# A 128x64-tiled key turn, a reordered kv sum and an earlier mantissa step in a fused polysketch attention and GELU block

## The chip, the cores and the metric

The kernel runs on one core of a Trainium2 chip. The metric is the device time of one execution in microseconds, a median over several runs. The engines of the core work side by side, each through its own instructions in order: TensorE (PE: matmuls; PEld is its loading of weights), VectorE (DVE), ScalarE (ACT), GpSimd (POOL) and SyncE (SP), which issues most of the DMAs. Matmul results land in PSUM, from where ACT and DVE take them.

## The reference

The reference is a polysketch attention followed by a GELU block. Only what bears on the change is shown:

```python
def phi(x):                                   # x: 4 batches, 4 heads, 1088 tokens, 32
    a = np.einsum('rd,bhsd->bhsr', S1, x)     # sketch, r = 8
    b = np.einsum('rd,bhsd->bhsr', S2, x)
    return np.einsum('bhsi,bhsj->bhsij', a, b).reshape(*x.shape[:-1], r * r)
q_p, k_p = (phi(q), phi(k))
kv = np.einsum('bhsf,bhsd->bhfd', k_p, v)
z = np.sum(k_p, axis=2)
num = np.einsum('bhsf,bhfd->bhsd', q_p, kv)
den = np.einsum('bhsf,bhf->bhs', q_p, z)[..., None] + 1e-06
x = num / den                                 # then (4352, 128): heads side by side
h = x @ w_in                                  # 128 x 2048
g = 0.5 * h * (1.0 + erf(h * inv_sqrt2))
out = g @ w_out                               # 2048 x 128
```

The reference returns float32. Some inputs (S1, S2 and both weights) arrive in 64-bit floating point, and the kernel makes their float32 values from the two 32-bit words itself.

## The kernel before

**Tiling.** The 1088 tokens of a batch are 1024 main tokens (8 groups of 128) and a remainder of 64. The four batches' main tokens make eight chunks of 512 tokens, the four remainders a ninth, shorter one. Each chunk goes through 16 hidden tiles of 128 channels: a product with w_in (line 721), a GELU on ACT (line 728), and the products with w_out (line 858 for the first tiles of the first batch, line 807 in a form with fewer products for all later ones).

**Staging.** The program is written out in order: for each engine, the order of the text is the order of its instructions, and the framework adds waits on semaphores where one engine needs another's result. A first part, lines 892 to 961, brings the first batch as far as its first hidden products. A loop over steps then runs the hidden tiles, and hangs all later preparation (rounding of weights, keys and queries of later batches) onto given steps. The change touches the first part alone.

**What the first part does, in order.** The sketches S1 and S2 are made. Keys of batch 0 are turned, so that their dimensions lie on partitions, and multiplied by the sketch (`key_features`). The four heads go as two pairs, r = 0 and r = 1, and each pair's features are `k_p[0, r]`. DVE multiplies three of the four halves of the features, POOL one; POOL also copies the values v into a wider tile `v_aug[r]` with a column of ones (lines 345 and 351), so that kv and z come out of one sum. The first queries are expanded (line 543), copied by ACT (line 550) and multiplied by DVE (line 555).

Then the sum over tokens, kv, is built in one PSUM bank, `kv_bank`. `kv_first(ps, r, tokens)` (line 426) issues two products for each group of tokens, each with 64 columns of weights, one for the upper and one for the lower 64 rows of the bank. Line 917 sums four of the eight groups of the first head pair. Line 918 turns the remainder's keys (`key_turn_rem`, which calls `transposed`, line 333, and copies by ACT, line 335, into `kT_rem`). Line 919 sums the other four groups. Line 920 multiplies `kT_rem` by the sketch (line 408), copies one factor by ACT (line 412, `a_rem`) and multiplies by DVE (line 413, `k_p_rem`). Line 921 sums all eight groups of the second head pair, and line 922 adds the remainder (line 432), which closes the sum. ACT copies it out as `kz` (line 930). `key_turn_rem` has a second use later in the loop, for the other pair of batches.

Around this, the second chunk's queries are turned (line 928, on TensorE through line 333). After kz, `numerators_by_token` (line 656) makes numerators and denominators of chunk 0, in two parts of two token groups each, and `divide` (lines 673 to 679) divides them on DVE. `turn_half_apart` (lines 694 and 696) turns the result into `xT`. `first_hidden` (line 737) is the first product with w_in, and the loop continues with the next hidden tiles (line 721).

**Rounding of weights.** A weight piece of 64-bit numbers is turned into float32 by the class `Rounding` in steps: `low_words` (ACT, line 260), `exponent_fields` (DVE, line 268), `mantissa_fields` (DVE, line 273), `exponents` (ACT, line 279), `mantissas` (DVE, line 287), `signs` (DVE, line 292), `product` (DVE or POOL, line 297). `fields` calls the exponent and the mantissa step one behind the other. Pieces 0 and 1 of w_in have 256 columns each: piece 0 serves the hidden tiles 0 and 1, piece 1 the tiles 2 and 3. POOL makes the product of piece 0, DVE that of piece 1. For piece 1 the exponent step stands at line 939, before the numerators, and the mantissa step at line 951, behind the copies of the turned x. When the product of piece 0 is done, POOL clears one word each of two landing tiles (line 180), on which SP's loads of w_out wait.

**PSUM.** Three pools of banks, each with two buffers: `h_ps` for hidden tiles, `o_ps` for outputs (in the first part `kv_bank` and the remainder's bank), `w_ps` for all else. A hidden tile's product can start only when the GELU has read the bank of the tile two before it.

Of the kernel before, what the change touches and what calls it, by code (L numbers as in the profile page):

```python
# [8 lines left out]
FP = mybir.dt.float32  # L9
# [7 lines left out]
def kernel(  # L17
# [18 lines left out]
    pe, dve, act, pool, sp = nc.tensor, nc.vector, nc.scalar, nc.gpsimd, nc.sync  # L36
# [7 lines left out]
    J = S // 128  # L44
# [16 lines left out]
    att = ctx.enter_context(tc.tile_pool(name="att", bufs=2))  # L61
# [18 lines left out]
    def out_bank():  # L80
        return ops.tile([128, CW], FP, name="o_ps")
# [8 lines left out]
    rem = {n: big.tile([128, B // 2, H, D], FP, name=f"{n}_rem") for n in "kv"}  # L90
# [128 lines left out]
    ident = big.tile([128, 128], FP, name="ident")  # L219
# [107 lines left out]
    def transposed(ps, name, srcs, copy, midway=lambda: None):  # L327

        n = len(srcs) * 128
        for i, s in enumerate(srcs):  # L330
            if 2 * i == len(srcs):
                midway()
            pe.transpose(ps[:, i * 128:(i + 1) * 128], in_=s, identity=ident)  # L333
        t = att.tile([128, n], FP, name=name, bufs=1 if name == "kT_rem" else 2)
        copy(out=t, in_=ps[:, :n])
        return t
# [5 lines left out]
    kT, k_p, k_p_rem = {}, {}, {}  # L342
# [27 lines left out]
    def spread(out, a, b):  # L370

        n = a.shape[1]
        return dict(out=out, in0=a[:, :, :, None].broadcast_to([128, n, R, R]),
                    in1=b[:, :, None, :].broadcast_to([128, n, R, R]))
# [25 lines left out]

    def key_turn_rem(pair, ps, copy):

        kT["rem"] = transposed(ps[:, 256:], "kT_rem", [rem["k"][:, pair].rearrange("p h d -> p (h d)")], copy)

    def key_features_rem(pair, ps):

        for rows in (slice(0, 64), slice(64, 128)) if pair == 0 else (slice(0, 128),):
            pe.matmul(ps[rows, 384:448], lhsT=kT["rem"][:, rows], rhs=S12.rearrange("p h r -> p (h r)"), start=True, stop=True)
        k_p_rem[pair] = big.tile([128, H, R, R], FP, name=f"k_p_rem{pair}")
        ab = ps[:, 384:448].rearrange("p (h r) -> p h r", r=2 * R)  # L410
        a = att.tile([128, H, R], FP, name="a_rem")
        act.copy(out=a, in_=ab[:, :, 0:R])
        dve.tensor_mul(**spread(k_p_rem[pair], a, ab[:, :, R:2 * R]))
# [3 lines left out]
    def flat(features):  # L417
        return features.rearrange("p i j -> p (i j)")

    def kv_first(ps, r, tokens=range(J)):  # L420

        for i in tokens:

            ch, t, one = i // 4, i // 2 % 2, i % 2
            for c in range(NP):
                pe.matmul(ps[c * F:(c + 1) * F, r * 2 * D:r * 2 * D + C], lhsT=flat(k_p[0, r][:, t, c * 4 + ch * 2 + one]),  # L426
                          rhs=v_aug[r][:, c, i, :C], start=(r == 0 and i == 0), stop=False, skip_group_check=True)

    def kv_first_rem(ps):
        for r in range(2):  # L430
            for c in range(NP):
                pe.matmul(ps[c * F:(c + 1) * F, r * 2 * D:r * 2 * D + C], lhsT=flat(k_p_rem[0][:, 2 * c + r]),
                          rhs=v_rem_aug[0][:, 2 * c + r, :C], start=False, stop=True, skip_group_check=True)
# [256 lines left out]
    def turn_half_apart(n, i, banks):  # L690
        if i == 0:
            xT[n] = att.tile([128, CW], FP, name="xT", bufs=3)
        for j, ps in enumerate(banks):
            pe.transpose(ps[:, :128], in_=x_tok[n, i][:, j].rearrange("p h d -> p (h d)"), identity=ident)
        for j, ps in enumerate(banks):
            (by_act, by_dve)[j](out=xT[n][:, i * 256 + j * 128:i * 256 + (j + 1) * 128], in_=ps[:, :128])
# [219 lines left out]
    kv_bank = out_bank()  # L916
    kv_first(kv_bank, 0, (0, 1, 4, 5))
    key_turn_rem(0, banks[1], by_act)
    kv_first(kv_bank, 0, (2, 3, 6, 7))
    key_features_rem(0, banks[1])  # L920
    kv_first(kv_bank, 1)
    kv_first_rem(kv_bank)
    w_in = [Rounding(w) for w in w_in_sb[:2]]
    w_in[0].low_words()
# [11 lines left out]
    w_out = [Rounding(w, beside=b) for w, b in zip(w_out_sb[:2], w_in)]  # L936
    by_act(**late[0])
    w_in[1].low_words()
    w_in[1].exponent_fields()
    parts = [range(2), range(2, JC)]  # L940
    nd = [[hidden_bank(), hidden_bank()], [out_bank(), out_bank()]]
    for banks, tokens in zip(nd, parts):
# [5 lines left out]
        divide(0, banks, tokens, by_head_pair=True, den=by)  # L948
    for half, bank in enumerate((hidden_bank, out_bank)):
        turn_half_apart(0, half, [bank(), bank()])  # L950
    w_in[1].mantissa_fields()
    for half in range(2):
        first_hidden(0, half)
    expand_copy(1, 0)
# [88 lines left out]
    def turn_keys_rem(pair):  # L1043
        held["rem"] = work_bank()
        key_turn_rem(pair, held["rem"], by_act)
# [46 lines left out]
    for n in range(3, NCHUNK):  # L1092
# [3 lines left out]
        keys = n % 2 and b < B  # L1096
# [158 lines left out]
```

## Time and profile before

| | |
|---|---|
| time, median of 3 runs | 259.67 us (258.98, 259.67, 259.85) |
| the profiled execution's own time | 259.66 us |
| its span, first to last instruction | 257.9 us |
| TensorE busy | 253.9 us (98%), 2335 matmuls |
| DVE, ACT, POOL busy | 151.1, 115.3, 164.6 us |
| mean granted TensorE clock | 1.000 |
| the first part (lines 892 to 961) on TensorE | up to about 16 us |

The span is what the profile covers; 1.8 us lie around it. A busy share counts the time between start and end of an engine's instructions. Matmuls overlap with the ones behind them and their ends are modelled, so the starts of matmuls tell more than their busy time: the distance between two starts is what one of them costs. In the views, a line gives start and length in us, then engine, line of the kernel, operation, what is written from what, shape and count; in brackets stands the idle time of the engine before it and who ended it.

### The profile page before, as it was taken

To read this page: it belongs to the slowest core of one execution; us is meant where nothing else is said; L and a number is where in the kernel's file an instruction comes from. 1 tells how busy PE (TensorE), PEld (TensorE's weight loads), DVE (VectorE), ACT (ScalarE), POOL (GpSimd) and SP (SyncE) were. 2 spreads that over 40 slices of the span, in tenths; PEclk is the share of its full clock that TensorE was granted. 3 is DMA by queue.
4 is the path that set the end of the run, shared out by engine and by line. 5 is a ranking of instruction groups with operands and counts; after the bars stand their busy time and mean duration, and the time that the engine had idled before them with its cause. 6 is when DMAs were issued, how large, how long until landed. Compare 5 with 4: busy or idle time off the path is not lost.

```text
span 257.9 us, 5770 instructions
## 1 busy us (share of the span) xinstructions
PE 253.9 (98%) x2335; PEld 135.7 (53%) x2335; DVE 151.1 (59%) x313; ACT 115.3 (45%) x224; POOL 164.6 (64%) x173
## 2 busy tenths in 40 slices
PE   8999999999999999999999999999999999999995
PEld 7856444354444545444444455455544444445794
DVE  2786888969699997590178986399307000700330
ACT  4675777433626332543335332533444334433442
POOL 3404016799968778587758775787758777877300
PEclk9999999999999999999999999999999999999999
DMA  7469849820000101102000002000200200020020
GB/s 204 140 188 373 201 94 220 221 55 10 3 0 13 30 1 23 21 8 35 3 0 3 0 10 37 0 1 3 41 3 5 38 0 1 10 34 0 3 41 20
DMA packets 29594, 13.48 MB, mean 52 GB/s; under 512 B 21888, under 2 KB 27776, under 8 KB 29568
## 3 DMA queue, kind: packets, MB, share of 16 engines
q1 hardware_dynamic: 29392, 13.05, 20.8%
q8 instruction: 18, 0.29, 0.5%
q10 hardware_dynamic: 176, 0.07, 0.1%
q14 instruction: 8, 0.07, 0.1%
HBM read 10.88 MB, written 2.23 MB: 51 GB/s over the span
## 4 chain that ended last, share of the span: by engine, by line
PE 98%; ACT 0%; issue 0%
PE h_ps L721 45%; PE o_ps L807 33%; PE o_ps L858 5%; PE w_ps L855 3%; PE w_ps L437 1%; PE w_ps L890 1%; PE w_ps L578 1%; PE w_ps L633 1%; PE w_ps L543 1%; PE o_ps L426 1%; PE h_ps L737 1%; PE w_ps L978 1%; PE w_ps L656 0%; PE h_ps L333 0%; PE w_ps L333 0%; PE o_ps L382 0%
## 5 line engine op out<-in xcount | busy, mean ns | idle before, releaser
L721 PE MATMUL h_ps<-xT,w_in 128*64 128x512 f32 (+3 forms) x514 | 137.0, 576 | 0.0
L728 ACT ACTIVATE block<-h_ps 128x512 f32<-128x512 f32 (+1 forms) x128 | 73.1, 571 | 117.3 <-PE h_ps L721 115.3
L721 PEld LDWEIGHTS h_ps<-xT,w_in 128*64 128x64 f32 (+1 forms) x514 | 41.8, 142 | 30.6 <-issue 11.6
L807 PE MATMUL o_ps<-block,w_out 128*64 128x256 f32 x224 | 57.5, 379 | 0.0
L772 POOL TENSOR_TENSOR bits_low<-block 128x512 f32<-128x512 f32 x28 | 35.9, 1282 | 27.8 <-ACT block L728 27.8
L807 PEld LDWEIGHTS o_ps<-block,w_out 128*64 128x64 f32 x224 | 30.5, 137 | 38.1 <-issue 27.6
L773 POOL TENSOR_TENSOR bits_a<-block 128x512 f32<-128x512 f32 x28 | 35.8, 1277 | 12.0 <-ACT block L728 11.9
L822 DVE COPY sums<-o_ps 64x256 f32<-64x256 f32 x8 | 3.3, 417 | 60.7 <-PE o_ps L807 60.7
L774 POOL TENSOR_TENSOR bits_e<-bits_a,block 128x512 f32<-128x512 f32 x28 | 36.1, 1288 | 2.2
L775 POOL TENSOR_TENSOR bits_m<-block,bits_e 128x512 f32<-128x512 f32 x28 | 35.9, 1280 | 2.2
L807 PE MATMUL o_ps<-bits_low,small 128*64 128x256 f32 x112 | 28.8, 379 | 0.0
L807 PE MATMUL o_ps<-block,small 128*64 128x256 f32 x112 | 28.8, 379 | 0.0
L807 PE MATMUL o_ps<-bits_a,small 128*64 128x256 f32 x112 | 28.8, 379 | 0.0
L807 PE MATMUL o_ps<-bits_m,w_out 128*64 128x256 f32 x112 | 28.7, 379 | 0.0
L807 PEld LDWEIGHTS o_ps<-block,small 128*64 128x64 f32 x112 | 15.2, 137 | 17.9 <-issue 10.8
L807 PE MATMUL o_ps<-bits_e,small 128*64 128x256 f32 x112 | 17.0, 383 | 0.0
L858 PE MATMUL o_ps<-g,w_out 128*128 128x512 f32 (+1 forms) x34 | 16.5, 572 | 0.0
L807 PEld LDWEIGHTS o_ps<-bits_m,w_out 128*64 128x64 f32 x112 | 15.3, 137 | 0.0
L807 PEld LDWEIGHTS o_ps<-bits_a,small 128*64 128x64 f32 x112 | 15.2, 137 | 0.0
L807 PEld LDWEIGHTS o_ps<-bits_low,small 128*64 128x64 f32 x112 | 15.2, 137 | 0.0
L590 DVE STREAM_TRANSPOSE w_ps<-w_ps 128x512 f32<-128x512 f32 (+1 forms) x7 | 4.8, 688 | 17.0 <-ACT xT L644 12.7
L807 PEld LDWEIGHTS o_ps<-bits_e,small 128*64 128x64 f32 x112 | 7.6, 137 | 10.6 <-issue 8.8
(195 smaller groups left out, 305.8 us busy)
## 6 DMA issues: line engine op xcount, KB each, us to landing
block<-in_moe_w_in_dram SPq DMA_DIRECT2D x3, 512.0 KB, 6.8
block<-in_moe_w_out_dram SPq DMA_DIRECT2D x3, 512.0 KB, 12.1
k<-in_k_dram SPq DMA_DIRECT2D x12, 128.0 KB, 2.9
v<-in_v_dram SPq DMA_DIRECT2D x12, 128.0 KB, 3.3
q<-in_q_dram SPq DMA_DIRECT2D x24, 64.0 KB, 2.3
out_dram<-oT SPq DMA_DIRECT2D x21, 64.0 KB, 2.2
k<-in_k_dram SPq DMA_DIRECT2D x2, 256.0 KB, 2.8
q<-in_q_dram SPq DMA_DIRECT2D x2, 256.0 KB, 3.8
```

The source lines that it names most:

```text
L426: pe.matmul(ps[c * F:(c + 1) * F, r * 2 * D:r * 2 * D + C], lhsT=flat(k_p[0, r][:, t, c * 4 + ch * 2 + one]), rhs=v_aug[r][:, c, i, :C], s ...
L590: dve.transpose(out=tok, in_=ps[:, :, :H2])
L721: pe.matmul(ps[rows, :W], lhsT=w[:, rows], rhs=xT[n][:, :W], start=True, stop=True)
L728: act.activation(out=g_of[n, fi][:, :W], in_=ps[:, :W], func=ACT.Gelu)
L772: pool.tensor_sub(out=s[3], in0=a11, in1=a21)
L773: pool.tensor_add(out=s[1], in0=a21, in1=a22)
L774: pool.tensor_sub(out=s[2], in0=s[1], in1=a11)
L775: pool.tensor_sub(out=s[4], in0=a12, in1=s[2])
L807: pe.matmul(acc[n][bank][half * 64:(half + 1) * 64, col:col + HW], lhsT=fixed, rhs=moving, start=opens and e == 0 and name in "4715", stop ...
L822: dve.tensor_copy(out=N[lo, 0, one], in_=a0[lo, one])
L855: pe.matmul(o_of[n][i][:, :128], lhsT=g[:, i * 128:(i + 1) * 128], rhs=w_tile(w_out_sb, fi), start=first, stop=final)
L858: pe.matmul(o_of[n][:, cols], lhsT=w_tile(w_out_sb, fi), rhs=g[:, cols], start=first, stop=final)
```

## The change

There are two edits in the first part, and one in a helper.

First, `mantissa_fields` of w_in's piece 1 moves on DVE from behind the copies of the turned x to just behind `exponent_fields`, which puts it ahead of the division of chunk 0.

Second, the first use of `key_turn_rem` (pair 0) no longer issues one transposing matmul of the whole 128x128 array. It issues two ordinary products with the identity, of 64 weight columns each, for the upper and the lower 64 rows of the bank. The copy by ACT stays. The later use (pair 1) stays as it was.

Third, four of the eight token groups of the second head pair's kv are summed before the remainder's sketch, and four behind it.

```diff
     def key_turn_rem(pair, ps, copy):
 
-        kT["rem"] = transposed(ps[:, 256:], "kT_rem", [rem["k"][:, pair].rearrange("p h d -> p (h d)")], copy)
+        keys = rem["k"][:, pair].rearrange("p h d -> p (h d)")
+        if pair:
+            kT["rem"] = transposed(ps[:, 256:], "kT_rem", [keys], copy)
+            return
+
+        for rows in (slice(0, 64), slice(64, 128)):
+            pe.matmul(ps[rows, 256:384], lhsT=keys[:, rows], rhs=ident, start=True, stop=True)
+        kT["rem"] = att.tile([128, 128], FP, name="kT_rem", bufs=1)
+        copy(out=kT["rem"], in_=ps[:, 256:384])
...
     key_turn_rem(0, banks[1], by_act)
     kv_first(kv_bank, 0, (2, 3, 6, 7))
+    kv_first(kv_bank, 1, range(4))
     key_features_rem(0, banks[1])
-    kv_first(kv_bank, 1)
+    kv_first(kv_bank, 1, range(4, J))
     kv_first_rem(kv_bank)
...
     w_in[1].low_words()
-    w_in[1].exponent_fields()
+    w_in[1].fields()
     parts = [range(2), range(2, JC)]
...
         turn_half_apart(0, half, [bank(), bank()])
-    w_in[1].mantissa_fields()
     for half in range(2):
```

## The prediction

> **What bounds the kernel.** I read first the chain of work that ended last and the busy time by stretches, then the timeline of the stretches that the edits touch. The page's chain:
>
> ```profile
> PE 98%; ACT 0%; issue 0%
> ```
>
> and one stretch (columns: us, then busy time of PE, PEld, DVE, ACT, POOL with instructions, PE's granted clock, DMA share, GB/s):
>
> ```profile
> 24.00:140.00 116.00, 116.00 (x953) 55.23 (x953) 85.58 (x158) 54.91 (x100) 80.24 (x79) 1.00 0.25 57
> ```
>
> TensorE sets the end, and from 24 us on it never runs dry. Both edits lie before 17 us, so the question is by how much TensorE's stream reaches 24 us earlier or later; the rest carries that offset. A busy PE can hide short waits, because matmuls overlap, so I go by their starts. The timeline around the first edit (start, length, engine, line):
>
> ```profile
> 8.66 0.66 PE L426 MATMUL o_ps<-sums,k_p 128*64 128x33 f32 x16
> ...
> 8.77 1.07 ACT L550 COPY A_sb<-w_ps 128x512 f32<-128x512 f32 x2 [0.61 <-PE w_ps L543]
> 9.14 0.61 POOL L345 COPY sums<-v 128x512 f32<-128x512 f32 x1
> ...
> 9.25 0.33 PE L333 MATMUL o_ps<-ident,k_rem 128*128 128x128 f32 x1
> ...
> 9.51 0.66 PE L426 MATMUL o_ps<-sums,k_p 128*64 128x33 f32 x16
> ...
> 9.73 0.28 ACT L335 COPY kT_rem<-o_ps 128x128 f32<-128x128 f32 x1
> ...
> 10.06 0.34 PE L408 MATMUL o_ps<-S,kT_rem 128*64 128x64 f32 x4
> ...
> 10.23 1.08 PE L426 MATMUL o_ps<-sums,k_p 128*64 128x33 f32 x32
> 10.45 0.19 ACT L412 COPY a_rem<-o_ps 128x32 f32<-128x32 f32 x1 [0.43 <-PE o_ps L408]
> ...
> 10.66 0.42 DVE L413 TENSOR_TENSOR k_p_rem<-a_rem,o_ps 128x256 f32<-128x256 f32 x1
> ...
> 11.23 0.42 PE L432 MATMUL o_ps<-v_rem_aug,k_p_rem 128*64 128x33 f32 x8
> ...
> 12.18 0.44 PE L656 MATMUL h_ps<-kz,q_pT 64*64 64x33 f32 x16
> ```
>
> See the sketch of the remainder at 10.06 (L408), its copy at 10.45, its product on VectorE at 10.66 to 11.08, and the kv product that needs it at 11.23 (L432). Then the copy kz, the numerators at 12.18, the division, the turn of x and the first hidden product at 15.07 follow, each on the one before.
>
> **The tiled turn.** Two 64-column products go in pairs: 16 pairs from 10.23 take 1.08, less the 0.22 of the last, over 15 pitches: 0.057 us a pair. Eight pairs from 8.66 are out of the way by 9.13, yet the turn starts at 9.25 and the next product at 9.51: with both changes of the array's tiling it costs 0.38. The new form, two 128x64 products with 128 moving columns, is not in this trace. A product is two MATMULs (16 for 8 calls at 8.66), a turn one. At line 543 a pass of 256 columns has a pitch of 0.215 (from 13.24, 1.12 less 0.37 for three pitches, the first longer), so 128 columns are 0.11 and two paired passes 0.22; bounds are 0.12 (33-column pairs, twice 0.057) and 0.44 (four passes not paired). I take 0.22, as the neighbours visibly pair; no change of tiling is left. TensorE gains 0.16 here (bounds -0.06 to 0.26): the second half of the first pair's kv starts at 9.35, not 9.51.
>
> The Trainium skill, "TensorEngine Tiling (Array Packing)", section "Restrictions", says that column tiling rules out the transpose mode for float32, which speaks against this edit. By that alone the turn doubles from 0.11 to 0.22, and the sum below would be 0.11 + 0.16 = 0.27 us worse than with my value; the two gaps around the turn in the row say why I don't go by it.
>
> Who profits? The copy kT_rem at 9.73 has its source at 9.58, but ScalarE's two A_sb copies run from 8.77 to 9.84 with an overlap: the copy goes when ScalarE is free. So kT_rem still lands at 10.01; the earlier turn brings the sketch nothing.
>
> **Half of the second pair's kv ahead of the sketch.** Eight pairs, 8 x 0.057 = 0.46. First half's rest from 9.35 to 9.81, then these eight to 10.27. Their inputs are there (v_aug by POOL at 9.14 + 0.61 = 9.75), with 0.06 to spare. But their first product waits on two engines, and a second wait is an instruction of its own in the weight queue: before L432, the 16 pairs from 10.23 end at 11.15 and the product starts at 11.23, 0.08 lost. Before the change this fell into the sketch's own wait; now it is paid, so the sketch goes at 10.35. The sketch's second pair, whose end frees the copy, was at 10.17 (0.057 before 10.23) and is now at about 10.41. So the sketch is **0.24 us later**. Bounds: 0.06 (turn at 0.12, no price for the wait) to 0.53 (unpaired turn, 0.22; POOL's copy 0.07 late).
>
> Queued behind it are ScalarE's copy a_rem (it waited for L408 at 10.45), the w_in steps behind that copy, the VectorE product L413 and all behind it. VectorE was free at 10.67, when L413 could start: there is no slack, all of it moves by 0.24, L432 to 11.47. TensorE has done the last eight pairs by 10.41 + 0.06 + 0.46 = 10.93 and then waits half a microsecond, where it waited 0.08. The query turn, kz, the numerators and the first hidden product move by the same 0.24; POOL's product of w_in's first piece too (12.44 + 0.75 = 13.19, needed at 15.07), and the gated loads that it holds on SP's queue, whose first result is used at 18.04.
>
> **The mantissa step** (L273) goes from behind the turned copies of x to just behind the exponent step, ahead of the division:
>
> ```profile
> 12.31 0.29 DVE L268 TENSOR_SCALAR bits_e<-small 128x256 uint32<-128x256 uint32 x1
> ...
> 12.89 0.23 DVE L673 TENSOR_SCALAR den_tok<-h_ps 128x4 f32<-128x4 f32 x2 [0.29 <-PE h_ps L656]
> ```
>
> VectorE idles 0.29 there for TensorE. One step started 0.20 behind L268 (11.00, 11.20) and takes 0.29: done at 12.80, before 12.89. It is hidden; without that cover the division would be up to 0.20 late. It waits for nothing new, since L268 read the same piece. What it leaves, and the weights that follow:
>
> ```profile
> 15.39 0.28 DVE L273 TENSOR_SCALAR bits_a<-small 128x256 uint32<-128x256 uint32 x1
> ...
> 15.70 0.42 DVE L287 SCALAR_TENSOR_TENSOR bits_m<-bits_a,bits_low 128x256 f32<-128x256 uint32 x1
> ...
> 16.03 2.99 PE L721 MATMUL h_ps<-xT,w_in 128*128 128x512 f32 x6
> ...
> 16.23 0.60 ACT L728 ACTIVATE g<-h_ps 128x512 f32<-128x512 f32 x1
> 16.50 0.42 DVE L297 TENSOR_TENSOR w_in<-bits_m,bits_e 128x256 f32<-128x256 f32 x1
> ...
> 17.04 0.30 PEld L721 LDWEIGHTS h_ps<-xT,w_in 128*128 128x128 f32 x2 [0.81 <-ACT g L728]
> ```
>
> w_in's second piece is ready at 16.92, and 0.31 earlier (15.70 - 15.39) after the change. The third hidden product waits for it: its weights load at 17.04 and it starts at 17.07, though the second, two passes of 0.43 from 16.03, was through at 16.89. It can't gain the whole 0.31: the bank it writes is free only when the first gelu ends, 16.23 + 0.60 = 16.83, and from there weights (0.05 behind a release, as L408 at 10.06 behind the copy's end at 10.01) and product (0.03) make 16.91. Gain **0.16** (bounds 0 and 0.23, the latter if also the slow restart after a wait went: 17.07 to 17.57 is 0.50 for a pass of 0.43). The later uses have cover: the query features end at 18.12 and are used at 18.95; w_out's first piece moves with VectorE, ahead of its use at 20.02.
>
> **Sum**, against the profiled execution: +0.24 - 0.16 = +0.08 us at 18 us and so at the end; bounds 0.06 - 0.23 = -0.17 and 0.53. Its span 257.9 becomes 258.0; what lies around it is 259.66 - 257.88 = 1.78, so 259.74. That execution is 0.01 below the median of the runs shown (259.67); I say **259.7**.
>
> **Rivals.**
> - *The remainder's chain has slack and TensorE keeps its gains*: 0.16 at the turn, 0.09 of wait before L408 (9.51 + 0.46 against 10.06), 0.08 before L432, 0.16 at the mantissa step: -0.49, 259.2. For it: the page shows no idle PE here. Against: the copy a_rem waited on L408 and L432 started 0.15 after VectorE's product.
> - *Unpaired turn, and the mantissa gains nothing*: +0.53, 260.2.
> - *Slower beyond doubt, by the clock*: the half microsecond of idle TensorE at 10.9 drops it to half speed. The trace shows such a speed: four 128-column turns take 1.06 from 3.78 and 0.66 from 11.59. It decides if the array falls back within 0.55 us; were it to stay so for the 5.7 us that the slow start lasts (0.77 to 6.47), half of them is lost: +2.9, 262.6. Against: waits of up to 0.18 pass here at full pitch.
>
> The Trainium skill, "TensorE: Matmul & The Clock Gate", Part 1, has the array go back to half rate only after a whole idle window of about 3.4 us. By it this rival is worth nothing; no run here shows the window.
>
> **Chances.** What a measurement can tell from no change is about 0.3%, 0.78 us; the three runs spread over 0.87, so that two medians may differ by it now and then. Forecast (259.7): 0.60, of it 0.05 reads faster and 0.04 slower by scatter. Slack: 0.22, of it 0.05 faster. Unpaired: 0.13, of it 0.03 slower. Clock: 0.05, slower. Faster 0.10, same 0.78, slower 0.12. The range reaches down past 259.2 by 0.3 of scatter and up past 260.2 by 0.3: 258.9 to 260.5.
>
> **What would show it.** Right: four MATMULs for the turn with the next kv product some 0.2 behind, L408 near 10.35, L432 near 11.47 behind an idle stretch, L273 ahead of the division, the third hidden product straight behind the second, and everything at 24 us within 0.2 of before. Wrong: L432 at or before 11.23, the division later than its numerators, or any new wait past 24 us.

## The result, and the profile after

| | before | after |
|---|---|---|
| median | 259.33 us (258.85 to 260.20, 22 runs) | 259.86 us (259.32 to 260.20, 22 runs) |
| the profiled execution's own time | 259.66 us | 260.2 us |
| its span | 257.9 us | 258.4 us |
| mean granted TensorE clock | 1.0 | 1.0 |

The ratio is 1.0016, with a 95% interval of 1.0009 to 1.0023: about 0.41 us slower (0.53 by the two medians), which is within 0.3% of no change. The changed kernel's profiled execution is the slowest of its 22. Of all executions in this study one was slow, 379.82 us at a granted clock of 0.66 in the combined kernel further down, and it is left out of that kernel's ratio. The forecast of 259.7 us lies 0.16 us below the measured median. The 22 runs of the kernel before have a median 0.34 us under that of the three runs shown at first, though, so against them the forecast difference of 0.08 us is short by some 0.33 us. That third of a microsecond is the subject of what follows.

In the changed kernel the lines from the sketch on are 8 higher (the sketch 408 is now 416, the kv products 426 are 434, the remainder 432 is 440, the denominators 673 are 681, the hidden products 721 are 729), and those from the new kv line to the old place of the mantissa step 9; the tiled turn is line 409 and its copy 411; lines below 400 keep their numbers.

The chain of work that ended last, in the changed kernel, by engine:

```profile
PE 95%; DMA 2%; DVE 0%; SPq 0%; ACT 0%; issue 0%
```

and the stretch from 24 to 140 us (busy time of PE, PEld, DVE, ACT and POOL, clock, DMA share, GB/s):

```profile
24.00:140.00 116.00, 116.00 (x952) 55.39 (x952) 85.37 (x159) 54.94 (x100) 79.25 (x79) 1.00 0.25 58
```

TensorE still never runs dry behind 24 us, and so the difference is made ahead of it. TensorE's timeline there:

```profile
8.81 0.66 PE L434 MATMUL o_ps<-sums,k_p 128*64 128x33 f32 x16
9.29 0.42 PE L409 MATMUL o_ps<-ident,k_rem 128*64 128x128 f32 x4
9.54 1.07 PE L434 MATMUL o_ps<-sums,k_p 128*64 128x33 f32 x32
10.45 0.32 PE L416 MATMUL o_ps<-S,kT_rem 128*64 128x64 f32 x4
10.59 0.61 PE L434 MATMUL o_ps<-sums,k_p 128*64 128x33 f32 x16
11.60 0.42 PE L440 MATMUL o_ps<-v_rem_aug,k_p_rem 128*64 128x33 f32 x8 [0.39 <-DVE k_p_rem L421]
```

The turn now is four MATMULs, and the next kv product follows 0.25 behind it. Sixteen pairs then stand ahead of the sketch instead of eight, and the remainder's kv product waits visibly for VectorE, which it did before for a moment only. The first kv product itself starts at 8.81 here and at 8.66 before. That start moves from one execution to the next with the landing of the inputs: over all profiles of this study it lies between 7.87 and 8.81. So the stages are counted from it here:

| us behind the first kv product | before | after | difference |
|---|---|---|---|
| sketch of the remainder | 1.406 | 1.639 | +0.233 |
| remainder's kv product | 2.573 | 2.788 | +0.215 |
| numerators | 3.516 | 3.729 | +0.213 |
| division | 4.236 | 4.803 | +0.567 |
| first hidden product | 6.407 | 6.874 | +0.467 |
| third hidden product | 8.410 | 8.763 | +0.353 |
| first hidden product past 24 us | 15.424 | 15.808 | +0.384 |
| end of the span | 249.220 | 249.592 | +0.372 |

This reads as two separate events. The key edits cost 0.21 and nothing more is added up to the numerators. Between numerators and division another 0.354 appears, of which 0.10 is absorbed by the first hidden product and 0.114 comes back at the third. The 0.372 at the end and the 0.15 by which the first kv product starts later make up the 0.5 us between the two profiled spans. The timeline of the other engines between numerators and division, where 0.354 is lost:

```profile
12.63 0.29 DVE L268 TENSOR_SCALAR bits_e<-small 128x256 uint32<-128x256 uint32 x1
...
12.80 0.73 POOL L297 TENSOR_TENSOR w_in<-bits_m,bits_e 128x256 f32<-128x256 f32 x1 [2.68 <-DVE bits_e L292]
12.84 0.85 DVE L273 TENSOR_SCALAR bits_a<-small 128x256 uint32<-128x256 uint32 x1
...
13.61 0.22 DVE L681 TENSOR_SCALAR den_tok<-h_ps 128x4 f32<-128x4 f32 x2
```

L273 is the moved mantissa step. At its old place it took 0.28 (line 273 at 15.39 in the profile before); here it takes 0.85, and shows no wait. It ends at 13.69, some 0.15 behind POOL's product, which began 0.04 ahead of it. The denominators (L681), the first step of the division, come behind the long instruction, where before they waited for TensorE. All of this is the reading of one execution of each kernel; the experiments ask whether it is the cause.

### The profile page after: what moved, and what is told of

Its sections match the earlier page's. It is cut to its first block, busy times and chain, and to the rows that moved or that the text cites. A ratio compares the mean times of both kernels' runs of the same rounds, so it can differ in the third digit from the quotient of the medians.

```text
span 258.4 us, 5777 instructions
## 1 busy us (share of the span) xinstructions
PE 253.3 (98%) x2338; PEld 135.7 (53%) x2338; DVE 151.5 (59%) x313; ACT 115.2 (45%) x224; POOL 163.5 (63%) x173
## 4 chain that ended last, share of the span: by engine, by line
PE 95%; DMA 2%; DVE 0%; SPq 0%; ACT 0%; issue 0%
PE h_ps L729 45%; PE o_ps L815 33%; PE o_ps L866 5%; PE w_ps L863 3%; DMA q<-in_q_dram 2%; PE w_ps L445 1%; PE w_ps L586 1%; PE w_ps L641 1%; PE w_ps L551 1%; PE h_ps L745 1%; PE o_ps L434 1%; PE w_ps L986 1%; PE w_ps L664 0%; SPq L100 0%; PE w_ps L333 0%; DVE qT L536 0%
```

## The experiments

Times are given as the median of the kernel, the ratio to the kernel before on the same chip and its 95% interval. An interval of 0.001 either way is 0.26 us, as large as most of what is asked for here; the traces resolve hundredths, but of one execution each. Both are given, and where they don't agree it is said.

**The parts alone.** Four kernels take the change apart. The first holds the key edits without the mantissa step, as against the changed kernel:

```diff
-    w_in[1].fields()
+    w_in[1].exponent_fields()
...
         turn_half_apart(0, half, [bank(), bank()])
+    w_in[1].mantissa_fields()
```

> The changed kernel with the mantissa step back in its old place; the turn in 128x64 tiles and the half kv sum ahead of the sketch stay. Times below are counted from the first kv product, since the two profiles reach it 0.15 us apart. In the changed kernel the remainder's kv product starts 0.215 us later than before, the numerators 0.213, and the first hidden product in steady order (at 24 us) 0.384. Theory K (the sketch moved back): remainder's kv product, numerators, division and first hidden product all 0.21 later than before, and 0.21 at 24 us; time about 0.2 us (0.08%) above before. Rival (all of the loss is the mantissa step's, the key edits cost nothing once the division is not disturbed): 0.0 to 0.05 at 24 us, time as before.

The second holds the mantissa step alone, as against the kernel before:

```diff
-    w_in[1].exponent_fields()
+    w_in[1].fields()
...
-    w_in[1].mantissa_fields()
```

> The kernel before with the mantissa step moved ahead of the division and nothing else. In the changed kernel that step took 0.852 us where it takes 0.282 in its old place, and it ran from 12.84 to 13.69 beside POOL's product of w_in's first piece, 12.80 to 13.54. Theory L (VectorE and POOL shut each other out there): here too the step takes 0.75 to 0.9 us and ends some 0.15 behind POOL's product, the division starts 0.3 to 0.4 later than before, and 0.15 to 0.2 stays at 24 us: time 0.06% above before. Rival D (in the changed kernel the step was long because the key edits had pushed it into something else, or because its input came late): here it takes 0.28 to 0.30, the division starts as before, and 0.16 us is gained at 24 us, as the prediction had it.

The third has the tiled turn, with the old order of the kv sums and the mantissa step at its old place (against the changed kernel):

```diff
-    kv_first(kv_bank, 1, range(4))
     key_features_rem(0, banks[1])
-    kv_first(kv_bank, 1, range(4, J))
+    kv_first(kv_bank, 1)
```

> The kernel before with the remainder's turn in two 128x64 tiles, and nothing else: all of the second pair's kv behind the sketch. In the changed kernel the turn and its next product came 0.085 us closer than before. Theory K: the sketch still waits for ScalarE's copy of the turned keys, which waits for ScalarE's two copies before it; sketch within 0.02 of before, remainder's kv product within 0.03, 24 us within 0.03, time as before. Rival (the tiled turn itself costs or gains on the path): remainder's kv product 0.05 or more away from before, and the same at 24 us.

The fourth has the new order with the old turn (against the kernel before):

```diff
+    kv_first(kv_bank, 1, range(4))
     key_features_rem(0, banks[1])
-    kv_first(kv_bank, 1)
+    kv_first(kv_bank, 1, range(4, J))
```

> The kernel before with four token groups of the second pair's kv ahead of the sketch, the turn in one transposing product, and nothing else. Theory K: the sketch comes 0.30 us later (0.213 as in the changed kernel and the 0.085 that the tiled turn gave back there), and so do the remainder's kv product, the numerators and the hidden products; time 0.3 us (0.12%) above before. Rival (the later sketch is absorbed behind it): the remainder's kv product later by 0.2 or more, but under 0.1 left at 24 us.

Differences to the kernel before, in us from the first kv product, and the times:

| | sketch | numerators | division | first hidden | third hidden | past 24 us | time, ratio (95%) |
|---|---|---|---|---|---|---|---|
| key edits alone | +0.428 | +0.407 | +0.407 | +0.406 | +0.405 | +0.405 | 259.47, 1.0002 (0.9992 to 1.0012) |
| mantissa step alone | +0.001 | -0.001 | +0.344 | +0.244 | +0.131 | +0.160 | 259.31, 0.9995 (0.9985 to 1.0004) |
| tiled turn alone | -0.014 | -0.013 | -0.013 | -0.012 | -0.011 | -0.011 | 259.41, 0.9995 (0.9974 to 1.0017) |
| order alone | +0.397 | +0.376 | +0.375 | +0.375 | +0.377 | +0.378 | 259.74, 1.0009 (1.0000 to 1.0018) |

The tiled turn is worth nothing by itself, as there was nothing behind it that could use the time. The order alone costs 0.38 and the changed kernel's numerators 0.21: the tiled turn gives 0.164 back once the order is such that TensorE's stream decides when the sketch goes (the second pair's first kv product stands 1.336 behind the first kv product with the old turn and 1.172 with the new one, in the changed kernel).

The mantissa step alone makes the division 0.344 late, with numerators that start at the same place to 0.001. VectorE and POOL in that kernel:

```profile
11.88 0.73 POOL L297 TENSOR_TENSOR w_in<-bits_m,bits_e 128x256 f32<-128x256 f32 x1 [2.47 <-DVE bits_e L292]
11.92 0.84 DVE L273 TENSOR_SCALAR bits_a<-small 128x256 uint32<-128x256 uint32 x1
...
12.68 0.22 DVE L673 TENSOR_SCALAR den_tok<-h_ps 128x4 f32<-128x4 f32 x2
```

Again POOL begins 0.04 ahead of L273, and L273 ends 0.15 behind POOL. So it is the mantissa step itself, and not the key edits around it, that makes the division late. This trace also holds a pause of TensorE inside the numerators (last section); a pause of that size put the division 0.145 late in another run, and the repeat of this one, without a pause, has the division 0.363 late.

The key edits alone gave +0.41 where the changed kernel has +0.21. Its timeline says why (TensorE, and POOL's copy of the second pair's values v):

```profile
8.04 0.66 PE L434 MATMUL o_ps<-sums,k_p 128*64 128x33 f32 x16
...
8.72 0.61 POOL L345 COPY sums<-v 128x512 f32<-128x512 f32 x1
8.78 1.27 PE L434 MATMUL o_ps<-sums,k_p 128*64 128x33 f32 x32
...
9.87 0.31 PE L416 MATMUL o_ps<-S,kT_rem 128*64 128x64 f32 x4
```

POOL's copy ends at 9.33, 1.29 behind the first kv product; in the changed kernel's profile it ended 1.09 behind it. The second pair's first product was due at 1.172 and went at 1.346, 0.05 behind the copy; in a later run with the copy at 1.375 it went at 1.428, again 0.05 behind. So the new order also brings a dependence on that copy into the chain, and in executions where the copy is late another 0.2 to 0.3 is paid. A repeat shows that it comes and goes:

> The key edits alone a second time, for a second profile and more times. In the first one TensorE reached the first kv product 0.6 us earlier than in the profile before, and there the second pair's kv waited for POOL's second copy of v. Theory K with POOL's copy: 0.21 at 24 us where POOL's copy is through before the second pair's kv begins, up to 0.41 where it isn't; time 0.2 to 0.4 us above before (0.08% to 0.16%). Rival (the delay from the first kv product is made up at the end, as the first times, 259.47 against 259.52, would have it): no difference in time again.

The repeat had the sketch at +0.233 and the numerators at +0.211, exactly as the changed kernel (259.55 us, 1.0010, 1.0001 to 1.0018). It lost another 0.45 inside the numerators, of which more below, and so stood at +0.67 past 24 us. The first run's time, within 0.31 of the kernel before by its interval, also suggests that its +0.405 in the trace isn't what most executions pay.

**How much can stand ahead of the sketch.** Two of the second pair's groups instead of four, without the mantissa step:

```diff
-    kv_first(kv_bank, 1, range(4))
+    kv_first(kv_bank, 1, range(2))
     key_features_rem(0, banks[1])
-    kv_first(kv_bank, 1, range(4, J))
+    kv_first(kv_bank, 1, range(2, J))
```

> Tiled turn, with two token groups of the second pair's kv ahead of the sketch and six behind it, mantissa step in its old place. In the changed kernel with four groups the sketch started 1.639 us after the first kv product, before it 1.406 behind ScalarE's copy; a group takes 0.117. Theory K (the sketch is late by what stands ahead of it beyond that copy): two groups end at 1.639 - 0.233 = 1.406, so the sketch starts within 0.03 of before, or up to 0.15 later where POOL's second copy of v is late; the remainder's kv product and 24 us likewise, 0.0 to 0.05 (0.15). Rival (any kv product of the second pair ahead of the sketch costs the whole): 0.2 or more.

Sketch, remainder and numerators are at -0.001 each (259.55 us, 1.0008, 0.9993 to 1.0023; a pause inside the numerators, as in the repeat above, put the rest at +0.14). None ahead gives -0.014 (+0.001 in the combined kernel below), two groups -0.001, four +0.233: TensorE has room for two groups while ScalarE's copies run, and the other two are on the chain in full (four pairs of 0.057, 0.23).

**Is it POOL's product that holds the mantissa step?** If it is, L273 must take its 0.28 when the product can't start ahead of it. A copy of one word of the step's result on POOL, just ahead of the product, makes the product follow it. First with the mantissa step alone, then with the whole change (the diff is against the changed kernel; the loads behind the product move with it):

```diff
     w_in[0].signs()
+    by_act(**late[0])
+    w_in[1].low_words()
+    w_in[1].fields()
+    pool.tensor_copy(out=mark, in_=w_in[1].a[:1, :1].bitcast(FP))
     w_in[0].product(pool)
     load_w_out(0, gated=True)
     load_rest()
     w_out = [Rounding(w, beside=b) for w, b in zip(w_out_sb[:2], w_in)]
-    by_act(**late[0])
-    w_in[1].low_words()
-    w_in[1].fields()
```

> The kernel before with the mantissa step moved ahead of the division, and POOL's product of w_in's first piece held back until that step is done (POOL copies one word of the step's result first; the gated loads stay behind the product). In the run with the mantissa step alone the step took 0.842 us and the division started 0.344 later, counted from the first kv product. Theory L (the two shut each other out while POOL's product runs): the step takes 0.28 to 0.30 again, the division starts within 0.03 of before, the first hidden product too, the third hidden product starts 0.15 earlier and 0.12 to 0.20 is gained at 24 us; POOL's product ends near 4.9 us after the first kv product, ahead of its use at 6.4. Theory D (the step is long by itself in that place): it stays at 0.8 us and the loss of 0.16 at 24 us stays.

> The changed kernel with POOL's product of w_in's first piece held back until the moved mantissa step is done. Theory L with K: the key edits' share stays (0.21 us at the numerators, up to 0.41 where POOL's second copy of v is late, counted from the first kv product), the division starts with the numerators again, and the third hidden product and 24 us are 0.15 earlier than with the key edits alone: 0.05 to 0.25 above before. Theory D: 0.38 or more above before at 24 us, as in the changed kernel.

VectorE and POOL with the mantissa step alone and the product held (one line more ahead of them, so that the step is L274 and the product L298):

```profile
11.83 0.28 DVE L274 TENSOR_SCALAR bits_a<-small 128x256 uint32<-128x256 uint32 x1
...
12.18 0.18 POOL L937 COPY mark<-bits_a 1x1 f32<-1x1 f32 x1 [2.65 <-DVE bits_a L274]
...
12.32 0.72 POOL L298 TENSOR_TENSOR w_in<-bits_m,bits_e 128x256 f32<-128x256 f32 x1
12.34 0.23 DVE L674 TENSOR_SCALAR den_tok<-h_ps 128x4 f32<-128x4 f32 x2 [0.23 <-PE h_ps L657]
```

The step takes 0.285, and the division waits for TensorE again, not for VectorE. What runs beside the product now are the division's instructions, the first at 0.23, as they did in the kernel before (L673 at 12.89 inside POOL's 12.44 to 13.19). So it is not any VectorE work that the product stretches.

| | sketch | numerators | division | first hidden | third hidden | past 24 us | time, ratio (95%) |
|---|---|---|---|---|---|---|---|
| mantissa step, product held | -0.014 | -0.013 | +0.080 | +0.079 | -0.098 | -0.075 | 259.34, 0.9996 (0.9987 to 1.0004) |
| whole change, product held | +0.510 | +0.490 | +0.490 | +0.536 | +0.361 | +0.385 | 259.45, 1.0003 (0.9994 to 1.0011) |

In the second of them POOL's copy of v was late again (1.375 behind the first kv product), which puts the numerators at +0.49. From there it tells the same: the division adds 0.000, where the changed kernel adds 0.354, and the third hidden product is 0.129 earlier than the numerators' place says. The first row's division is late by 0.09 through a pause inside the numerators.

A second way to take the cause away leaves the order and cuts the product in two, as against the changed kernel:

```diff
-    w_in[0].product(pool)
+    for c in (slice(0, 128), slice(128, 256)):
+        pool.tensor_mul(out=w_in_sb[0][:, c], in0=w_in[0].m[:, c], in1=w_in[0].e.bitcast(FP)[:, c])
```

> The changed kernel with POOL's product of w_in's first piece issued as two products of 128 columns each. Theory L, with the two shutting each other out for a whole instruction: the mantissa step waits only for the first half (some 0.4 us long), takes 0.45 to 0.6 where it took 0.852, and POOL's second half waits for it and ends later; the division starts 0.2 to 0.3 earlier than in the changed kernel, counted from the numerators. Theory D (late data, other traffic): the step stays near 0.85 whatever POOL's product looks like. If the two share the access instead of excluding each other, the step takes 0.8 as well, and both halves are stretched.

Its VectorE and POOL:

```profile
12.65 0.92 POOL L943 TENSOR_TENSOR w_in<-bits_m,bits_e 128x128 f32<-128x128 f32 x2 [2.67 <-DVE bits_e L292]
12.69 0.57 DVE L273 TENSOR_SCALAR bits_a<-small 128x256 uint32<-128x256 uint32 x1
...
13.18 0.22 DVE L681 TENSOR_SCALAR den_tok<-h_ps 128x4 f32<-128x4 f32 x2
```

The halves took 457 and 506 ns, the first from 12.65 to 13.10. L273 ends at 13.25, 0.15 behind the first half, though the second runs on to 13.57. So it waits for the POOL instruction that was there first, to its end, and then goes. The two don't share at a lower speed: POOL's whole product takes 0.73 to 0.74 with the step beside it (0.78 in one repeat) and 0.72 to 0.75 without, and a straight line through POOL's 0.73 for 256 columns and 1.28 for 512 gives 0.455 for 128 (an estimate), about what the first half took. The division is 0.074 late instead of 0.354, the third hidden product 0.142 early against the numerators, and past 24 us the kernel stands at +0.100 (259.46 us, 1.0004, 0.9995 to 1.0012).

**The version without both losses.** The tiled turn, the old order of the kv sums, the early mantissa step and the held product together:

```diff
-    kv_first(kv_bank, 1, range(4))
     key_features_rem(0, banks[1])
-    kv_first(kv_bank, 1, range(4, J))
+    kv_first(kv_bank, 1)
...
     w_in[0].signs()
+    by_act(**late[0])
+    w_in[1].low_words()
+    w_in[1].fields()
+    pool.tensor_copy(out=mark, in_=w_in[1].a[:1, :1].bitcast(FP))
     w_in[0].product(pool)
...
-    by_act(**late[0])
-    w_in[1].low_words()
-    w_in[1].fields()
```

> The parts that cost nothing, put together: the turn in 128x64 tiles with the sketch where it was before (all of the second pair's kv behind it), the mantissa step ahead of the division, and POOL's product of w_in's first piece held back until that step is done. Theories L and K: sketch and remainder's kv product as before or 0.014 earlier, mantissa step 0.28 to 0.30, third hidden product 0.15 to 0.2 earlier and 0.14 to 0.18 gained at 24 us, counted from the first kv product (0.075 in the run with the product held alone, in which TensorE paused for 0.08 amid the numerators with no wait that the trace shows); time 0.05% to 0.07% under before. Rival (the two edits disturb each other): nothing gained at 24 us, or a loss.

Its VectorE, POOL and TensorE (lines one higher than in the changed kernel again):

```profile
12.24 0.28 DVE L274 TENSOR_SCALAR bits_a<-small 128x256 uint32<-128x256 uint32 x1
...
12.66 0.23 DVE L682 TENSOR_SCALAR den_tok<-h_ps 128x4 f32<-128x4 f32 x2
12.73 0.74 POOL L298 TENSOR_TENSOR w_in<-bits_m,bits_e 128x256 f32<-128x256 f32 x1
...
14.83 1.13 PE L746 MATMUL h_ps<-xT,w_in 128*128 128x128 f32 x8
```

All stages up to the first hidden product stand within 0.003 of the kernel before, the third hidden product at -0.173 and the work past 24 us at -0.150. The time is 259.09 us against 259.37 (ratio 0.9989, 0.9978 to 0.9999), the only kernel here whose whole interval lies below the kernel before. The held product ends 0.52 later than in the kernel before (5.05 behind the first kv product, not 4.53), and the loads of w_out behind it with it; TensorE past 24 us is busy throughout here as well, so that cost nothing. The gain is still less than 0.3%, and was measured once: the ratio puts it at 0.29 us and the trace at 0.15, and of a dozen intervals one can lie to one side by chance.

**Repeats.** The mantissa step alone and the changed kernel, each once more, beside the kernel above:

> The mantissa step alone a second time. Theory L: the step takes 0.84 again, 0.14 to 0.18 lost at 24 us from the first kv product; time 0.15 us (0.06%) above before. Rival (the step's wait for POOL depends on chance): 0.28 this time and a gain.

> The changed kernel again, on the same chip as its two parts. Theories L and K: the loss at 24 us is the sum of the key edits' (0.21 to 0.41) and the mantissa step's (0.16), less what they share: 0.35 to 0.57 from the first kv product; the step takes 0.85; time 0.3 to 0.5 us above before. Rival (the parts don't add up, and the loss is a third thing): the loss of the whole differs from the sum of the two parts' in this call by more than their intervals.

The mantissa step alone again has an L273 of 0.825 and a division 0.363 later than its numerators; past 24 us it stands at +0.129. Its time is 259.33 us, 0.9997 (0.9980 to 1.0013). The changed kernel again has L273 at 0.871, the division 0.377 later than its numerators, and +0.402 past 24 us; its time is 259.56 us, 1.0012 (1.0004 to 1.0021), so +0.19 by the medians and +0.31 by the ratio, beside the +0.41 of the 22 runs.

One thing stays open here. The two traces of the mantissa step alone stand at +0.160 and +0.129, but its times don't show it: the first run's interval ends at +0.10 us and has its middle below nothing. That L273 is stretched and the division late is shown by every trace in which the product starts ahead of it; that the step alone makes the kernel's time longer is not shown.

## Why the prediction was right, and where it was wrong

**What bounds the kernel**: right. An offset made before 24 us is carried to the end: +0.384 there, +0.372 at the span's end.

**The tiled turn**: right in its gain of 0.16, measured as 0.164 between the changed kernel and the one with the order alone. Of that, 0.113 is there when the first pair's second half starts (0.849 behind the first kv product with the old turn, 0.736 with the new); the rest is the first step behind it, from one pair to the next, 0.079 with the old turn and 0.029 with the new. The two passes stand 0.139 apart, nearer to the 0.11 of a paired pass than to the 0.215 of one for itself, and the gaps for the change of tiling are gone. That the earlier turn brings the sketch nothing by itself is what the turn alone shows (-0.014).

**Half of the second pair's kv**: the mechanism was right, a chain without slack behind the sketch, and the sum nearly: 0.24 forecast, 0.213 measured at the numerators. Two terms in it were off, one against the other. The price of 0.08 for a second wait was not paid: the second pair's first product follows 0.436 behind the start of the first pair's second half, where eight pairs of 0.057 take 0.46. And that second half started 0.74 behind the first kv product, not 0.69. What the range held as POOL's copy 0.07 late turned out larger: it put the sketch 0.20 and 0.28 later (0.428 and 0.510, less 0.233) in two of the seven profiles with four groups ahead.

**The mantissa step**: wrong, and this is the step that failed. "It is hidden" looked for a free slot on VectorE alone, found 0.29 us of it, and counted a step of 0.28. The timeline of before already showed POOL at its product from 12.44 to 13.19, right across that slot, but POOL was only asked when its result was needed:

```profile
12.44 0.75 POOL L297 TENSOR_TENSOR w_in<-bits_m,bits_e 128x256 f32<-128x256 f32 x1 [2.46 <-DVE bits_e L292]
```

In place of the hidden step the runs show one of 0.83 to 0.87 that ends 0.15 to 0.17 behind POOL's instruction. The fallback price, "up to 0.20 late", was too small as well (0.354 measured), because it took the step's length as given.

The profile of the kernel before also held the effect itself, further on. The steps L268 and L273 have twice the columns there and take 0.42 with POOL out of the way (L273 at 28.29). At 42 us both begin inside an instruction of POOL:

```profile
40.89 1.28 POOL L297 TENSOR_TENSOR w_in<-bits_m,bits_e 128x512 f32<-128x512 f32 x1 [2.64 <-DVE bits_e L292]
41.95 0.51 DVE L268 TENSOR_SCALAR bits_e<-block 128x512 uint32<-128x512 uint32 x1
42.13 0.64 POOL L759 TENSOR_TENSOR small<-w_out 128x128 f32<-128x128 f32 x1
42.38 0.68 DVE L273 TENSOR_SCALAR bits_a<-block 128x512 uint32<-128x512 uint32 x1
```

Each ends 0.28 behind the end of the POOL instruction that it began in (42.17 and 42.77). So do all five of this width that began inside one in that profile; the others kept 0.41 to 0.42. What is left behind POOL's end is 0.28 with 512 columns and 0.15 with 256, so it grows with the data, as a pass over the data that only starts when POOL is through would.

The Trainium skill, "SBUF — State Buffer", section "Who interferes with whom", has the rule that speaks against the move: a tensor_scalar on VectorE in a two-port mode shares a pair of ports with GpSimd, and whichever of them issues first keeps the pair for its whole instruction while the other is blocked entirely. The runs agree with it in both respects: the block ends with the first POOL instruction (0.57 with halves, 0.85 with the whole), and there is none with POOL behind (0.285). That L273 runs in such a mode is taken from the rule; no run here shows it. The trace of before shows a speed: twice the columns cost this step 0.14 more (0.28 to 0.42), and L287, which has two inputs, 0.27 more (0.42 at 15.70, 0.69 at 28.82).

**The gain at the third hidden product**: right. The forecast was that w_in would be ready in time and the bank, free when the first gelu ends, would set the start. The timeline after shows it (columns as above):

```profile
16.88 0.42 DVE L297 TENSOR_TENSOR w_in<-bits_m,bits_e 128x256 f32<-128x256 f32 x1
16.89 0.63 ACT L736 ACTIVATE g<-h_ps 128x512 f32<-128x512 f32 x1
...
17.57 0.30 PEld L729 LDWEIGHTS h_ps<-xT,w_in 128*128 128x128 f32 x2 [0.74 <-ACT g L736]
```

w_in's piece is there at 17.30, the gelu ends at 17.52, and the weights load 0.05 behind it. The gain is 0.114 in the changed kernel, 0.142 with the product in halves and 0.176 with it held, where 0.16 was forecast. So the sum +0.24 - 0.16 had both its terms; what it lacked was the division's +0.354, of which 0.10 was absorbed ahead of the first hidden product: 0.213 + 0.354 - 0.100 - 0.114 = 0.353 at the third hidden product. Another 0.02 to 0.03 up to 24 us appears in every kernel with the early mantissa step and in none without it. It lies between the two passes of the third hidden product, 0.504 apart before and 0.523 to 0.534 apart with the early step; why is open.

**The rivals.** The remainder's chain has no slack (where the sketch is late, the numerators are late by the same to within 0.03, in every run). The clock stayed: TensorE idles ahead of L440, 0.39 us by its line, at a granted clock of 1.0, and the eight products behind it take the 0.42 they took before. The rival of an unpaired turn came close in size, +0.53 against +0.41, by a mechanism that isn't there.

**The signs, and luck.** Two of the signs that the prediction had set itself went against it: the division came later than its numerators (0.354), and the work at 24 us stood 0.384 from before, not within 0.2. That 259.7 still came within 0.16 of the measured median is luck in good part: the three runs that it started from had a median 0.34 above the larger sample's, and that made up for the 0.33 that the forecast difference fell short.

## What to carry to other kernels

A free slot is free only if every engine that shares something with the instruction is looked at for the length of the slot: a VectorE step of this kind that begins inside a GpSimd instruction can last as long as that one, and its record shows a longer instruction and no wait. Whether a step is of this kind the profile of the kernel at hand can tell, where the same line already runs beside that engine. Where such a step is moved, order the two so that the short one goes first, or cut the long one. Work moved ahead of a serial chain is free only up to the time for which the chain waits on another engine anyway; here two groups fitted and four cost 0.21 us, and a tiling that saves TensorE time pays only when TensorE is what that point waits for.

## What was not expected of the hardware

**TensorE pauses with no wait on record.** In four kernels (the mantissa step alone, the same with its product held, two groups ahead, and the second run of the key edits) TensorE stopped inside the first numerators, ahead of the 21st or the 24th of their 32 MATMULs. TensorE in the repeat of the key edits:

```profile
12.11 0.54 PE L664 MATMUL h_ps<-kz,q_pT 64*64 64x33 f32 x20
12.88 0.36 PE L664 MATMUL h_ps<-kz,q_pT 64*64 64x33 f32 x11 [0.23 <-issue]
```

The bracket names "issue", which is time in which the engine waited for nothing that the profile shows. At that place 0.11 to 0.45 lie between the starts of two neighbours, where 0.06 is the most in the other ten profiles (in the changed kernel's all 32 start within 0.45). The pause was worth 0.14 past 24 us in one run and 0.46 in another, as much as anything else in this study. In all four, TensorE resumed 2.28 to 2.40 us after the first packet of a 16 KB transfer on the queue for instructions; the profiles without a pause came to this place 2.39 us or more after that packet. That points to code that arrives late, but it is a correlation: no run moved the transfer, and the cause stays open.

**VectorE blocked looks like VectorE busy.** The 0.57 us that L273 waits for POOL counts in the busy time of VectorE and is no idle time in any view. Only the length of one instruction against its usual one shows it; the answer for line 273 in the changed kernel has the shortest, the median and the longest of its two up to 16 us (ns):

```profile
L273 DVE TENSOR_SCALAR bits_a<-small x2: 289/570/852, 11.6 to 12.8; 128x256 uint32<-128x256 uint32 x2
```

The same holds in the other direction for POOL: the clearing of two words (L180), which takes 0.12 for the two in the kernel before, took 0.25 where it fell beside L273's end.
